# Second-half scores with both heads on 128 partitions, and batch 0's first queries turned on TensorE

## The chip, the cores and the metric

The kernel runs on one core of a Trainium2 chip. The metric is the device time of one execution in microseconds, median of the runs. Of the core's engines TensorE (PE) multiplies matrices into PSUM, VectorE (DVE) and ScalarE (ACT) work on PSUM and SBUF, GpSimd (POOL) on SBUF alone; SyncE (SP) issues most DMAs and all DMA transposes.

## The reference

Attention over 4 batches, 8 heads, 576 positions and 64 columns per head, with a decay from cumulated logarithms of f and a causal mask, then two feed-forward layers over 2304 tokens:

```python
scores = scale * np.matmul(q, k.transpose(0, 1, 3, 2))
cum = np.cumsum(np.log(np.clip(f, 0.0001, 1.0)), axis=-1)
scores = np.where(causal, -1000000000.0, scores + cum[..., :, None] - cum[..., None, :])
attn = np.exp(scores - scores.max(-1, keepdims=True))
x = (attn / (attn.sum(-1, keepdims=True) + 1e-09)) @ v      # heads side by side: 2304 x 512
h = x @ w_in; x = np.maximum(0.01 * h, h) @ w_out           # 512 -> 2048 -> 512
h = x @ w2_in                                               # 512 -> 1024
solu = h * softmax(h)
ln = (solu - mean) / np.sqrt(var + 1e-06) * g_ln
out = ln @ w2_out                                           # 1024 -> 512
```

The weights come in eight bytes per number.

## The kernel before, in words

**Precision.** The feed-forward layers and P·V multiply float16 pairs: each operand is split into a high and a low half, and three products (high·high, high·low, low·high) are summed in PSUM. Scores of a head's first 256 queries ("A" passes, query blocks 0 and 1) are plain float32 matmuls of 66 or 68 rows: 64 of q or k and 2 or 4 of decay. Scores of the other queries ("B" passes: blocks 2 and 3 of 128 queries, and block 4 with the last 64 queries of both heads side by side) use the one-pass type float32r on values split in high and low parts.

**Work of a pair.** A pair is two heads of a batch; there are 16. `prep_full` (L605) loads q and k of an A pass with its decay rows from the DRAM table `dr_d`, in four small DMAs; for batch 0 they are in the tile `qa` from the start. `prep_split` (L621) loads q and k for a B pass with both heads on 128 partitions, and makes for each head two operand tiles `kq`: high parts of one head on one half of the partitions, copies or low parts on the other half, so that one 128-row matmul sums two products, and a 68-row one sums the third and the decay. That takes five copies and subtractions on 64 partitions per head, of 960, 576, 576, 384 and 384 columns. `scores` (L759) multiplies into a `ps_s` bank and takes the row maximum with the mask on VectorE; `softmax` (L717) has ScalarE write exp and its sum, takes the reciprocal, writes float16 halves `hl` of the probabilities, and transposes them by DMA into `pt` (`turn`, L507, on SP). `pv` (L819) multiplies with the float16 halves of V (`split_v`, L692), `evac` (L805) adds the two halves' results into `xr`, and `pair` (L848) splits `xr` into `x`.

**Feed-forward.** Nine blocks of 256 tokens: blocks 0 to 3 are the batches' first 256 positions, 4 to 7 the next 256, 8 the last 64 of all four. A hidden product (`hidden`, L972) needs the block's four pairs in `x`; the output product needs the eight `WO` tiles of its weight group, which share one scale, found by `power` (L667) when all are in. Each weight is loaded into one of three `wst` buffers, joined from its 16-bit parts (L886), bounded and split.

**Order.** All operations go through a planner (`Plan.run`, L187), which lists them with engine, estimated duration, buffers and a due number, and deals them out to the engines in that order when operands and buffers are free; operations with several possible engines get the one that is free first. The program on each engine is the planner's list, and waits are semaphores. `PASSES` gives the due numbers of the A and B passes, `UN` and `ORDER` the order of feed-forward blocks, `LD`, `LDV` and `LDW` how far loads go ahead. There are four `ps_s` banks and one `ps_v` bank.

## Time and profile before

| | us |
|---|---|
| median of 3 runs | 770.1 (768.19 to 773.19) |
| the profiled execution | 769.71 |
| its span, first to last instruction | 767.9 |
| PE busy | 707.0 (92%) |
| DVE, ACT, POOL busy | 529.8, 455.6, 285.0 |

The span is cut into stages below: up to 18 us there are loads and set-up, from 18.0 us scores, from 71.26 us the feed-forward beside attention, from 410 us feed-forward alone.

### The profile page before, as it was taken

How to read it: one execution, taken by the hardware profiler on the slowest of the kernel's cores; microseconds unless marked ns; L12 is line 12 of the kernel's file. 1: busy time of each engine (PE TensorE's matmuls, PEld its weight loads, DVE VectorE, ACT ScalarE, POOL GpSimd, SP SyncE). 2: the span in 40 equal slices, each digit the busy share in tenths (PEclk: the TensorE clock that was granted, in tenths of full speed). 3: DMA queues.
4: the chain of work that ended last, by engine and by line, in shares of the span. 5: the costliest groups of instructions: out<-in, count | busy, mean ns of one | idle time of the engine just before them, and what ended most of it. 6: DMA issues, size and time to landing. Idle time of an engine off the chain costs nothing.

```text
span 767.9 us, 15495 instructions
## 1 busy us (share of the span) xinstructions
PE 707.0 (92%) x5657; PEld 536.9 (70%) x5657; DVE 529.8 (69%) x1343; ACT 455.6 (59%) x1084; POOL 285.0 (37%) x408
## 2 busy tenths in 40 slices
PE   0465889999999999999999999999999999999997
PEld 0244767788888888888889888888875444444443
DVE  6888988776887887677776775212126887778762
ACT  2687999894998779989986576122222332222221
POOL 4546888681766056545551154000002111110110
...
GB/s 239 223 271 207 126 225 210 145 83 139 157 147 144 122 134 130 126 138 131 177 135 115 202 156 29 28 1 15 15 1 83 101 107 109 110 111 82 76 76 82
DMA packets 164139, 94.16 MB, mean 123 GB/s; under 512 B 144368, under 2 KB 144576, under 8 KB 164064
## 3 DMA queue, kind: packets, MB, share of 16 engines
...
q14 instruction: 31, 0.25, 0.1%
...
## 4 chain that ended last, share of the span: by engine, by line
PE 58%; ACT 2%; DMA 2%; DVE 1%; issue 0%; SPq 0%; POOL 0%; ACTq 0%; DVEq 0%
PE ps_f L511 38%; PE ph L511 12%; PE ps_g L511 3%; PE ps_s L511 3%; PE ps_v L511 2%; DMA pt<-hl 1%; ACT ps_s L724 1%; DMA raw<-w2i 1%; ACT hl L465 0%; ACT ps_f L987 0%; ACT xr L808 0%; ACT kq L465 0%; DVE hl L476 0%; ACT ot L1125 0%; ACT junk L662 0%
## 5 line engine op out<-in xcount | busy, mean ns | idle before, releaser
L511 PEld LDWEIGHTS <-wz 128*128 128x128 f16 x2808 | 272.0, 98 | 38.0 <-issue 5.8
L511 PE MATMUL ps_f<-g,wz 128*128 128x256 f16 x780 | 100.8, 273 | 0.0
L476 DVE SCALAR_TENSOR_TENSOR hl<-ps_s,st,hl 128x512 f16<-128x512 f32 (+4 forms) x160 | 82.2, 539 | 22.1 <-ACT hl L465 20.5
L511 PE MATMUL ps_f<-dec,wz 128*128 128x256 f16 x732 | 96.6, 276 | 0.0
L511 PE MATMUL ph<-wy,y 128*128 128x512 f16 x432 | 95.9, 379 | 0.0
L1099 POOL TENSOR_SCALAR s<-s 128x1 f32<-128x1 f32 x18 | 3.4, 190 | 234.5 <-DVE s L1094 215.3
L724 ACT ACTIVATE ps_s<-ps_s,st 128x512 f32<-128x512 f32 (+4 forms) x160 | 78.5, 491 | 19.6 <-DVE st L777 15.6
L480 POOL TENSOR_TENSOR kq<-raw,kq 64x576 fp32r<-64x576 f32 x64 | 77.2, 1209 | 14.0 <-ACT kq L465 8.1
L511 PEld LDWEIGHTS <-tr 128*128 128x128 f16 x432 | 41.9, 98 | 51.4 <-DMA tr<-hl 1.3
L465 ACT ACTIVATE hl<-ps_s,st 128x512 f16<-128x512 f32 (+4 forms) x150 | 73.2, 527 | 7.2 <-DVE st L745 2.6
L511 PEld LDWEIGHTS <-y 128*128 128x128 f16 x432 | 42.1, 98 | 50.3
L511 PE MATMUL ps_v<-pt,VT 128*128 128x128 f16 (+1 forms) x928 | 59.8, 216 | 17.3 <-DMA pt<-hl 8.8
L511 PE MATMUL ps_f<-x,wz 128*128 128x256 f16 x576 | 70.5, 276 | 0.6 <-DVE dec L988 0.6
L511 PEld LDWEIGHTS <-VT 128*128 128x128 f16 x928 | 52.5, 100 | 25.2 <-DMA pt<-hl 10.7
L777 DVE CUSTOM_DVE_ANT_0 ps_s<-ps_s,mask 128x128 f32<-128x128 f32 (+3 forms) x128 | 62.5, 495 | 10.7 <-PE ps_s L511 9.1
L511 PEld LDWEIGHTS <-qa 128*128 128x128 f16 x648 | 62.6, 98 | 8.2 <-issue 0.9
L511 PE MATMUL ps_s<-kq 128*128 128x512 f32 (+5 forms) x256 | 62.1, 369 | 2.7 <-DVE hl L476 2.5
L1082 ACT ACTIVATE raw<-ph,s,ex 128x1024 f32<-128x1024 f32 x18 | 21.6, 1201 | 68.7 <-DVE s L1081 68.0
L988 DVE TENSOR_TENSOR g<-ps_f,g 128x512 f16<-128x512 f32 x37 | 25.5, 689 | 45.4 <-ACT ps_f L987 45.0
L511 PE MATMUL ps_f<-wy,tr 128*128 128x512 f16 x234 | 54.8, 379 | 0.8 <-ACT ot L1125 0.8
L511 PE MATMUL ps_f<-sd,wz 128*128 128x256 f16 x360 | 49.2, 273 | 0.0
L511 PEld LDWEIGHTS ps_s<-kq 128*128 128x128 f32 (+1 forms) x256 | 41.4, 192 | 10.2 <-DVE hl L476 4.6
...
## 6 DMA issues: line engine op xcount, KB each, us to landing
...
VT<-vt SPq DMA_DIRECT2D x16, 320.0 KB
raw<-yp_d SPq DMA_DIRECT2D x18, 256.0 KB
...
out<-ot SPq DMA_DIRECT2D x16, 256.0 KB
raw<-kqa SPq DMA_DIRECT2D x12, 256.0 KB
```

The source lines that it names most:

```text
L465: nc.scalar.activation(o, i, CP, scale=1.0 if scale is None else scale)
L476: nc.vector.scalar_tensor_tensor(o, a, scale, b, op0=ALU.mult, op1=ALU.subtract)
L480: (nc.vector if eng == DVE else nc.gpsimd).tensor_tensor(o, a, b, op=ALU.subtract)
L511: nc.tensor.matmul(o, lhsT=l, rhs=r, start=start, stop=stop)
L724: P.op(ACT, act(W, 1, True) + 93, lambda view=view, j=j, k=k: nc.scalar.activation(view(), view(), AF.Exp, bias=sts.t[:, j:j + 1], scale=- ...
L777: P.op(DVE, dve(W) + 130, lambda i=i, j=j, view=view: nc.vector.tensor_tensor_reduce(view(), view(), mask[:, 512 - 128 * i:640], -0.125, 3 ...
L988: P.op(DVE, dve(512) + 60, lambda: nc.vector.tensor_tensor(g.t[:, 1], ps.t, g.t[:, 0], op=ALU.subtract), eprio, w=[(g, 1)], r=[ps, (g, 0)])
L1082: P.op(ACT, act(1024, 2, True), lambda: nc.scalar.activation(E(), ps.t, AF.Exp, bias=st.t[:, 0:1], scale=ev(SY + blk), accum_out=st.t[:, 1 ...
L1099: nc.gpsimd.tensor_scalar(st.t[:, 5:6], st.t[:, 5:6], 1.0e-6, 1.0, op0=ALU.add, op1=ALU.mult)
```

## The change

- `prep_split` makes one set of three tiles for both heads of a pair, on 128 partitions: high parts, low parts (each in two pieces, 576 and 384 columns), and the decay rows of each head at partitions 0 and 64 of the third tile, whose first 64 rows are zeroed at the start.
- `scores2` replaces `scores` for blocks 2 and 3: for both heads at once, four products (high·high, high·low, low·high, decay) of 64 rows, 4 rows for the decay, alternating between the heads, each head into its own bank. Block 4 takes the same four products on 128 rows.
- `turned` replaces `scores`, `softmax` and `pv` for batch 0's A pass: exp stays in float32 and unnormalised, TensorE multiplies it as stationary operand with a diagonal of the reciprocals, which turns and normalises it, the result is copied to SBUF, and P·V runs in float32 on the unsplit V straight into `x`. `split_v` of batch 0 moves behind its A pass.
- The table `dr_d` is turned by 256 columns, so that an A pass loads its decay rows in one DMA.
- Due numbers, engine choices, block order (`ORDER`, `UN`) and the planner's costs are set anew.

The diff, cut:

```diff
-ORDER = (0, 4, 1, 5, 3, 2, 8, 6, 7)
+ORDER = (0, 1, 4, 5, 3, 2, 6, 8, 7)
 EARLY = 1779.78
 NE = 4
-NQK = 3
+NQK = 2
+KH_ENGS = ("ACT", "DVE", "POOL")
+KL_ENGS = ("DVE", "POOL")
...
-PASSES = (("A", 0, 127.52, 0.5), ("A", 1, 186, 3), ("B", 0, 200, 5), ("A", 2, 222, 8), ("B", 1, 256, 20), ("A", 3, 338, 8), ("B", 2, 373.26, 20), ("B", 3, 454.38, 15.2))
+PASSES = (("A", 0, 127.52, 0.5), ("A", 1, 162.84, 3), ("B", 0, 200, 3.07), ("A", 2, 222, 8), ("B", 1, 234.49, 20), ("A", 3, 338, 8), ("B", 2, 373.26, 20), ("B", 3, 454.38, 15.2))
...
-LD = 11.72
-LDV = 18.49
-LDW = -17.77
+LD = 10.04
+LDV = 8.66
+LDW = -32.78
...
-WSP = (122.0, 192.0)
+WSP = (109.84, 192.0)
...
-UN = ((0, 0), (1, 0), (0, 1), (1, 1))
+UN = ((0, 0), (1, 0), (0, 1), (4, 0), (1, 1), (4, 1))
...
+PTB = (0,)
+DG_ENGS = ("ACT", "DVE", "POOL")
+TE_ENGS = ("ACT", "DVE")
...
+        for k in P.tags["qk"].free:
+            nc.gpsimd.memset(k[2][0:64].bitcast(F32), 0.0)
...
         load((bq, 0), lambda: a(0, 64), lambda: kqa[p].rearrange("(h d) c -> d h c", h=2), 64 * 1024 * 4, prio - LD)
-        for hd in range(2):
-            for c0, k0 in ((0, 0), (256, KB)):
-                load((bq, (hd, c0)), lambda hd=hd, c0=c0: a(64, 68)[:, hd, c0:c0 + 256], lambda hd=hd, k0=k0: dr_d[row(hd, p), :, k0:k0 + 256], 4096, prio - LD,
-                     deps=st["cols"])
-        QK[p] = [[bq]] * 2, lambda hd: a(0, 68)[:, hd], {0: 256, 1: 384}
+        load((bq, 1), lambda: a(64, 68), lambda: dr_d[2 * KD:].rearrange("(h p) t c -> p t h c", h=2)[p - KD, :, :, 0:512], 16384, prio - LD, deps=st["cols"])
+        QK[p] = [[bq]] * 2, lambda hd: a(0, 68)[:, hd], {0: 0, 1: 128}
 
     def prep_split(p, prio):
 
 
-        bufs = []
         N = KB
-        raw = P.buf("raw")
+        raw, bq = P.buf("raw"), P.buf("qk")
         load(raw, lambda: raw.t[:, 0:N], lambda: kq[p, :, 0:N], 128 * N * 4, prio - LD)
         for hd in range(2):
-            bq = P.buf("qk")
-            bufs.append(bq)
-            own, oth = (slice(64 * x, 64 * x + 64) for x in (hd, 1 - hd))
-            T = lambda n, r, c, d, bq=bq: bq.t[n][r, c:d]
-            R = lambda c, d, own=own: raw.t[own, c:d]
-            top = slice(0, 64)
-            copy_f(lambda T=T, own=own: T(0, own, 0, N), lambda R=R: R(0, N), N, prio + PP, w=[(bq, 0)], r=[raw])
-            sub_f(lambda T=T: T(1, top, 0, S), lambda R=R: R(0, S), lambda T=T, own=own: T(0, own, 0, S).bitcast(F32), S, prio + PP,
-                  w=[(bq, "k2")], r=[raw, (bq, 0)])
-            copy_f(lambda T=T, oth=oth: T(0, oth, 0, S), lambda T=T, own=own: T(0, own, 0, S).bitcast(F32), S, prio + PP,
-                   w=[(bq, "k0")], r=[(bq, 0)])
-            copy_f(lambda T=T: T(1, top, S, N), lambda T=T, own=own: T(0, own, S, N).bitcast(F32), N - S, prio + PP,
-                   w=[(bq, "q2")], r=[(bq, 0)])
-            sub_f(lambda T=T, oth=oth: T(0, oth, S, N), lambda R=R: R(S, N), lambda T=T, own=own: T(0, own, S, N).bitcast(F32),
-                  N - S, prio + PP, w=[(bq, "q0")], r=[raw, (bq, 0)])
-            load((bq, "d"), lambda bq=bq: bq.t[1][64:68, 0:N].bitcast(F32), lambda hd=hd: dr_d[row(hd, p), :, 0:N], 16 * N, prio - LD, deps=st["cols"])
-        QK[p] = [[b] for b in bufs], lambda hd: bufs[hd].t, {2: CQ, 3: CQ + 128, 4: CL}
+            load((bq, ("d", hd)), lambda hd=hd: bq.t[2][64 * hd:64 * hd + 4, 0:N].bitcast(F32), lambda hd=hd: dr_d[row(hd, p), :, 256:256 + N],
+                 16 * N, prio - LD, deps=st["cols"])
+        for c, d in ((0, S), (S, N)):
+            copy_f(lambda c=c, d=d: bq.t[0][:, c:d], lambda c=c, d=d: raw.t[:, c:d], d - c, prio + PP, engs=KH_ENGS, w=[(bq, (0, c))], r=[raw])
+            sub_f(lambda c=c, d=d: bq.t[1][:, c:d], lambda c=c, d=d: raw.t[:, c:d], lambda c=c, d=d: bq.t[0][:, c:d].bitcast(F32), d - c, prio + PP,
+                  engs=KL_ENGS, w=[(bq, (1, c))], r=[raw, (bq, (0, c))])
+        QK[p] = [[bq]] * 2, lambda: bq.t, {2: CQ, 3: CQ + 128, 4: CL}
...
-    def split_v(b, prio):
+    def scale_v(b, prio):
         power(EV + 5 * b, KD + 1, [(EX, ("v", KD * b + i)) for i in range(KD)], EB + b, ("b", b), prio)
         inverse(XS + b, ev(EB + b), ("x", b), ("b", b), prio)
+
+    def split_v(b, prio):
...
+    PROD = ((0, 0), (0, 1), (1, 0), (2, 2))
+
+    def qk_both(Q, i, os, k1):
+        _, qk, col = Q
+        t, c0 = qk(), col[i]
+        for n, (x, y) in enumerate(PROD):
+            for hd in range(2):
+                r = slice(64 * hd, 64 * hd + (4 if x == 2 else 64))
+                mm(os[hd], t[x][r, c0:c0 + 128], t[y][r, 0:k1], n == 0, n == 3)
...
+    def scores2(p, i, prio):
+
+        W, pss = 128 * (i + 1), [P.buf("ps_s") for _ in range(2)]
+        P.op(PE, 4 * mmr(W), lambda Q=QK[p]: qk_both(Q, i, [ps.t[:, 0:W] for ps in pss], W), prio, w=pss, r=QK[p][0][0])
+        pts = []
+        for hd, ps in enumerate(pss):
+            sts, view = P.buf("st"), lambda ps=ps: ps.t[:, 0:W]
+            P.op(DVE, dve(W) + 130, lambda sts=sts, view=view: nc.vector.tensor_tensor_reduce(
+                view(), view(), mask[:, 512 - 128 * i:640], -0.125, 3.0e38, ALU.add, ALU.min, sts.t[:, 0:1]), prio + KSTEP * hd, w=[(sts, 0)], rw=[ps])
+            pts.append({i: (softmax([(view, sts, 0, W, [(0, W, 0, W)], ps)], prio + KSTEP * hd), 0)})
+        return pts
...
             def pe(ps=ps, k0=k0, k1=k1, Q=QK[p]):
-                for hd in range(2):
-                    qk_mm(Q, full, 4, ps.t[:, 0:k1 - k0], hd, k0, k1, hd == 0, hd == 1)
+                t, c0 = Q[1](), Q[2][4]
+                for n, (x, y) in enumerate(PROD):
+                    r = slice(0, 68 if x == 2 else 128)
+                    mm(ps.t[:, 0:k1 - k0], t[x][r, c0:c0 + 128], t[y][r, k0:k1], n == 0, n == 3)
 
             n = k1 - k0
-            P.op(PE, 8 * n / 2.4 if full else 4 * mmr(n), pe, prio, w=[ps], r=bq[0] + bq[1], heat=HEAT if full else 1.0)
+            P.op(PE, 4 * mmr(n), pe, prio, w=[ps], r=QK[p][0][0])
...
+    def turned(p, hd, xs, ps_x, prio):
+
+        sts, ps, h = P.buf("st"), P.buf("ps_s"), P.buf("hl")
+        b, kd = divmod(p, KD)
+        vr = RAW[p]
+        f32 = lambda t: (t if len(t.shape) == 2 else t.rearrange("p a n -> p (a n)")).bitcast(F32)
+        at, wide = (0, 128), (128, 256)
+        for i in range(2):
+            P.op(PE, 4 * wide[i] / 2.4, lambda i=i, Q=QK[p]: qk_mm(Q, i, ps.t[:, at[i]:at[i] + wide[i]], hd, 0, wide[i], True, True), prio,
+                 r=QK[p][0][hd], heat=HEAT, w=[(ps, i)])
+        for i in range(2):
+            view = lambda i=i: ps.t[:, at[i]:at[i] + wide[i]]
+            P.op(DVE, dve(wide[i]) + 130, lambda i=i, view=view: nc.vector.tensor_tensor_reduce(
+                view(), view(), mask[:, 512 - 128 * i:640], -0.125, 3.0e38, ALU.add, ALU.min, sts.t[:, i:i + 1]), prio, w=[(sts, i)], rw=[(ps, i)])
+        for i in range(2):
+            P.op(ACT, act(wide[i], 1, True) + 93, lambda i=i: nc.scalar.activation(
+                f32(h.t)[:, at[i]:at[i] + wide[i]], ps.t[:, at[i]:at[i] + wide[i]], AF.Exp, bias=sts.t[:, i:i + 1], scale=-1.0, accum_out=sts.t[:, 3 + i:4 + i]),
+                prio, w=[(sts, 3 + i), (h, i)], r=[(ps, i), (sts, i)])
+
+        def guard():
+            for i in range(2):
+                nc.vector.tensor_scalar(sts.t[:, 6 + i:7 + i], sts.t[:, 3 + i:4 + i], 1.0e-9, None, op0=ALU.add)
+
+        P.op(DVE, 140, guard, prio, w=[(sts, 6)], r=[(sts, 3), (sts, 4)])
+        P.op(DVE, 75, lambda: nc.vector.reciprocal(sts.t[:, 9:11], sts.t[:, 6:8]), prio, w=[(sts, 9)], r=[(sts, 6)])
+        dg, pt, pst = P.buf("pt"), P.buf("pt"), P.buf("ps_f")
+        for i in range(2):
+            copy_f(lambda i=i: f32(dg.t)[:, 128 * i:128 * i + 128], lambda: ident.bitcast(F32), 128, prio, engs=DG_ENGS, scale=lambda i=i: sts.t[:, 9 + i:10 + i],
+                   w=[(dg, i)], r=[(sts, 9)])
+
+        def swap():
+            for i, j, c in ((0, 0, 0), (1, 0, 128), (1, 1, 256)):
+                k = at[i] + 128 * j
+                mm(pst.t[:, c:c + 128], f32(h.t)[:, k:k + 128], f32(dg.t)[:, 128 * i:128 * i + 128], True, True)
+
+        P.op(PE, 3 * 4 * 128 / 2.4, swap, prio + PTP, w=[pst], r=[h, dg], heat=HEAT)
+        copy_f(lambda: f32(pt.t)[:, 0:384], lambda: pst.t[:, 0:384], 384, prio, engs=TE_ENGS, psum=True, w=[pt], r=[pst])
+
+        def pe():
+            for i, j, c in ((0, 0, 0), (1, 0, 128), (1, 1, 256)):
+                mm(ps_x.t[:, 256 * hd + 128 * i:256 * hd + 128 * i + 128], vr.t[:, 128 * j:128 * j + 128], f32(pt.t)[:, c:c + 128], j == 0, j == i)
+
+        P.op(PE, 3 * 4 * 128 / 2.4, pe, prio + AV, w=[(ps_x, hd)], r=[vr, pt], heat=HEAT)
+        x, o, rows = xs[0], xs[1], slice(64 * hd, 64 * hd + 64)
+        src = lambda: ps_x.t[rows, 256 * hd:256 * hd + 256]
+        sc, key = lambda: ev(XS + b)[rows], [(EX, ("x", b))]
+        copy_f(lambda: x.t[rows, 0, o:o + 256], src, 256, prio + AV, engs=TE_ENGS, scale=sc, psum=True, w=[(x, (0, kd, hd))], r=[(ps_x, hd)] + key)
+        sub_f(lambda: x.t[rows, 1, o:o + 256], src, lambda: x.t[rows, 0, o:o + 256], 256, prio + AV, engs=(DVE,), scale=sc, psum=True,
+              w=[(x, (1, kd, hd))], r=[(ps_x, hd), (x, (0, kd, hd))] + key)
...
+        if full and b in PTB:
+            if len(XB.setdefault(b, [])) == kd // 2:
+                XB[b].append(P.buf("x"))
+            ps_x = P.buf("ps_v")
+            for hd in range(2):
+                turned(p, hd, (XB[b][kd // 2], TB * (kd % 2)), ps_x, prio + SM + KSTEP * hd)
+            attn_ops.extend(P.ops[n0:])
+            return
         xr = P.buf("xr")
         k = 0
-        for hd in range(2):
-            pts = {}
-            for unit in UNITS[len(blocks)]:
-                pts.update(scores(p, unit, hd, prio + SM + KSTEP * k, full))
-                k += 1
-            pv(p, hd, pts, xr, prio + AV)
-            if hd == HD4 and 4 in blocks:
-                pv4(p, scores4(p, prio + SM + KSTEP * k, full), xr, prio + AV)
-                k += 1
+        if full:
+            for hd in range(2):
+                pv(p, hd, scores(p, (0, 1), hd, prio + SM + KSTEP * hd), xr, prio + AV)
+        else:
+            both = [{}, {}]
+            for k, i in enumerate(U3):
+                for pts, new in zip(both, scores2(p, i, prio + SM + 2 * KSTEP * k)):
+                    pts.update(new)
+            if not HD4:
+                pv(p, 0, both[0], xr, prio + AV)
+            pt4 = scores4(p, prio + SM + 4 * KSTEP)
+            if HD4:
+                pv(p, 0, both[0], xr, prio + AV)
+            pv(p, 1, both[1], xr, prio + AV)
+            pv4(p, pt4, xr, prio + AV)
...
-                split_v(b, at + PV)
+                scale_v(b, at + PV)
+                if b not in PTB:
+                    split_v(b, at + PV)
             for i in range(KD):
                 pair(KD * b + i, at + step * i, (0, 1) if k == "A" else (2, 3, 4))
+            if k == "A" and b in PTB:
+                split_v(b, at + PV)
```

## Rows read from the trace of the kernel before

**Rows 1.** The page, part 1: busy time, share, instructions.
```profile
PE 707.0 (92%) x5657; PEld 536.9 (70%) x5657; DVE 529.8 (69%) x1343; ACT 455.6 (59%) x1084; POOL 285.0 (37%) x408
```
**Rows 2.** Stages: stretch, length; busy PE, PEld, DVE, ACT, POOL; PEclk, DMA share, GB/s.
```profile
0.00:18.00 18.00, 0.47 (x1) 0.31 (x2) 11.28 (x23) 5.03 (x7) 8.43 (x20) 1.00 0.85 237
18.00:71.26 53.26, 26.98 (x104) 19.15 (x105) 45.02 (x141) 37.75 (x110) 28.79 (x35) 1.00 0.91 251
71.26:110.00 38.74, 33.34 (x280) 27.64 (x279) 34.88 (x100) 36.83 (x90) 32.47 (x33) 1.00 0.56 152
110.00:150.00 40.00, 36.79 (x341) 31.23 (x340) 31.85 (x95) 36.58 (x86) 31.07 (x38) 0.96 0.80 195
...
190.00:410.00 220.00, 216.09 (x2120) 189.26 (x2119) 171.88 (x522) 194.90 (x512) 113.90 (x156) 1.00 0.69 142
```
**Rows 3.** Timeline of PE: start, length, what, count [idle before, releaser].
```profile
18.01 3.33 PE L511 MATMUL ps_s<-qa 66*128 66x128 f32 x10 [0.36 <-DMA qa<-sd]
...
32.38 1.65 PE L511 MATMUL ps_s<-qa 66*128 66x128 f32 x4 [3.23 <-DVE hl L476]
...
66.13 0.80 PE L511 MATMUL ps_v<-pt,VT 128*128 128x128 f16 x6 [0.98 <-DVE xr L811]
...
71.26 4.16 PE L511 MATMUL ps_f<-x,wz 128*128 128x256 f16 x24
...
89.75 5.40 PE L511 MATMUL ps_f<-g,wz 128*128 128x256 f16 x48
```
**Rows 4.** The chain that ended last: start, length, what.
```profile
283.87 2.62 PE ps_f L511 x24
```
**Rows 5.** Timeline of the SP queue: batch 1's decay loads, batch 0's last transposes.
```profile
22.97 6.71 SPq L502 DMA_DIRECT2D raw<-dr_d  x8
...
55.90 2.92 SPq L508 DMA_TRANSPOSE pt<-hl  x2
```
**Rows 6.** Timelines of DVE and ACT between the scores and the first hidden product.
```profile
55.85 0.73 DVE L476 SCALAR_TENSOR_TENSOR hl<-ps_s,st,hl 128x128 f16<-128x128 f32 x2
...
66.93 0.69 DVE L886 SCALAR_TENSOR_TENSOR wz<-wst,wk 128x512 int32<-128x512 int32 x1 [0.45 <-POOL wk L472]
...
70.08 0.15 DVE L654 TENSOR_REDUCE va<-ex 128x1 fp32r<-128x9 f32 x1
...
69.57 0.41 ACT L465 ACTIVATE x<-xr 128x256 f16<-128x256 f32 x1
```
**Rows 7.** Groups of DVE, 0 to 110 us: busy, mean ns, idle before.
```profile
L476 DVE SCALAR_TENSOR_TENSOR hl<-ps_s,st,hl 128x256 f16<-128x256 f32 x16 | 7.6, 475 | 0.2
...
L811 DVE SCALAR_TENSOR_TENSOR xr<-ps_v,xr 64x256 f32<-64x256 f32 x15 | 6.3, 420 | 4.0 <-ACT xr L808 3.8
```
**Rows 8.** Timeline of POOL in the set-up.
```profile
7.07 0.49 POOL L554 TENSOR_SCALAR sd<-sd 8x256 f32<-8x256 f32 x1 [0.71 <-DVE sd L553]
7.61 2.39 POOL L581 MEMSET dec<- 32x576 f32 x4
```
**Rows 9.** The tile kq alone, sum of stages 0 to 410 us, busy by engine.
```profile
sum 410.00, PE 61.54 PEld 41.13 DVE 0.81 ACT 34.35 POOL 113.42; mean PE 10.26 PEld 6.86 DVE 0.14 ACT 5.72 POOL 18.90
```
**Rows 10.** Groups of POOL and ACT that write kq, whole run.
```profile
L480 POOL TENSOR_TENSOR kq<-raw,kq 64x576 fp32r<-64x576 f32 x32 | 45.4, 1420 | 12.8 <-ACT kq L465 8.1 <-POOL st L741 2.6 <-DVE st L745 0.3
L480 POOL TENSOR_TENSOR kq<-raw,kq 64x384 fp32r<-64x384 f32 x32 | 31.9, 998 | 1.1
...
L465 ACT ACTIVATE kq<-kq 64x576 fp32r<-64x576 f32 x22 | 15.0, 682 | 0.7 <-POOL kq L472 0.2
```
**Rows 11.** Waits of PE, whole run, then 0 to 110 us: us, times, longest.
```profile
PE ps_s L511 <- DVE hl L476: 11.0, 9, 3.3
...
PE ps_s L511 <- DVE hl L476: 9.0, 5, 3.3
```
**Rows 12.** Timeline of weight loads (PEld) of a 64-column kq product.
```profile
99.40 0.52 PEld L511 LDWEIGHTS ps_s<-kq 128*128 128x128 f32 x4 [0.21 <-DVE hl L476]
```
**Rows 13.** The page, part 5: weight loads of kq, busy, mean ns.
```profile
L511 PEld LDWEIGHTS ps_s<-kq 128*128 128x128 f32 (+1 forms) x256 | 41.4, 192 | 10.2 <-DVE hl L476 4.6
```

More of the change, by code (lines that the diff above doesn't have):

```diff
@@ L63 @@
 NTR = 3
-YB_ENGS = ("DVE", "ACT")
+PTB = (0,)
+DG_ENGS = ("ACT", "DVE", "POOL")
+TE_ENGS = ("ACT", "DVE")
+PTP = 0.0
+PWL = 500.0
+DMAR = 320.0
+YB_ENGS = ("ACT",)
 VB_ENGS = ("DVE",)
 IB_ENGS = ("DVE",)
-OB_ENGS = ("DVE", "ACT")
-XP = -2.2
-XH_ENGS = ("ACT", "POOL")
+OB_ENGS = ("ACT",)
+XP = -8.31
+XH_ENGS = ("ACT", "DVE", "POOL")
 XL_ENGS = ("DVE", "POOL")
@@ L75 @@
 US0 = 20.0
-HST = 2.5
+HST = 2.59
 TB = 256
@@ L86 @@
 GS = 2.0 ** -24
-YD = 15.51
-OLAG = 33.39
+YD = 17.37
+OLAG = 40.32
 WSC = 256.0
@@ L113 @@
 class Op:
-    __slots__ = ("eng", "dur", "emit", "bufs", "prio", "npred", "succ", "seq", "taken", "dma", "weight", "heat", "lock")
-WEIGHT = {"DVE": 7.07}
-WEIGHT2 = {"DVE": 1.2}
+    __slots__ = ("eng", "dur", "emit", "bufs", "prio", "npred", "succ", "seq", "taken", "dma", "weight", "heat", "lock", "late")
+WEIGHT = {"DVE": 7.06}
+WEIGHT2 = {"DVE": 0.71}
 HEAT = 0.25
-TOPE = 267.42
+TOPE = 268.51
 QUEUES = ("SP",)
-SHARE = 0.54
+SHARE = 0.47
 PORT = 150.0
@@ L126 @@
 HI_ENGS = ("ACT", "DVE")
-UNITS = {2: ((0, 1),), 3: ((3,), (2,))}
+U3 = (3, 2)
 V_ENGS = ("ACT", "POOL")
@@ L194, in run @@
         warm, win, busy = False, 0, 0.0
-        port = 0.0
+        port, ends = 0.0, []
         def push(t, kind, x):
@@ L289, in run @@
                             continue
+                        if o.dma is not None and len(ends) >= 8 and ends[-8] > now:
+                            push(ends[-8], 0, None)
+                            skipped.append(item)
+                            break
                         if locks(o, e) and port > now + PORT:
@@ L333, in run @@
                         end = dma_free + 1000.0
+                        ends.append(end)
                     else:
@@ L338, in run @@
                     push(end, 1, o)
-                    push(end + TOPE, 2, o)
+                    push(end + TOPE + o.late, 2, o)
             if not left:
@@ L441, in body @@
     zrow = zcol.to_broadcast([32, S])
-    P.tag("qk", [tuple(ap.tile([128, KB], F32R, name=f"kq{n}_{j}") for j in range(2)) for n in range(NQK)])
+    P.tag("qk", [tuple(ap.tile([128, KB], F32R, name=f"kq{n}_{j}") for j in range(3)) for n in range(NQK)])
     P.tag("ps_f", tiles(psum, "ps_f", 3, [128, 512], F32))
@@ L501, in move @@
         d = {SP: 475.0, ACT: 490.0, POOL: 1040.0}
-        return flex(engs, [d[e] for e in engs], lambda e: queue[e].dma_start(dst(), src()), prio, dma=nbytes / 360.0, **kw)
+        return flex(engs, [d[e] for e in engs], lambda e: queue[e].dma_start(dst(), src()), prio, dma=nbytes / DMAR, **kw)
     def load(buf, dst, src, nbytes, prio, mode="w", **kw):
@@ L557, in decay @@
         bq = QA[0]
-        for k, r, x, c0 in (("n", 64, n8, 0), ("c", 65, c8, 256)):
+        for k, r, x, c0 in (("n", 64, n8, 256), ("c", 65, c8, 0)):
             move(lambda r=r, c0=c0: qa[r:r + 1, :, :, c0:c0 + 256].rearrange("r h p c -> r (h p) c"), x, 8192, pr,
@@ L579, in decay @@
             T(1, 0, S), c(), -8.0, T32(0, 0, S), op0=ALU.mult, op1=ALU.subtract), [hi])
-        for t, a, b in ((0, CQ, KQ), (1, CQ, KQ), (2, 0, S), (3, 0, S)):
-            step(t, POOL, 500.0, lambda t=t, a=a, b=b: nc.gpsimd.memset(T32(t, a, b), 1.0))
+        for t, a, b in ((0, CQ, KB), (0, KB, KQ), (1, CQ, KB), (1, KB, KQ), (2, 0, S), (3, 0, S)):
+            step(t, POOL, pool1(b - a), lambda t=t, a=a, b=b: nc.gpsimd.memset(T32(t, a, b), 1.0))
         for t in range(2):
@@ L593, in decay @@
                 two(T(t, CL, CQ)), T32(t - 2, 512, S).unsqueeze(1).to_broadcast([32, 2, 64]), -1.0, own(), op0=ALU.mult, op1=ALU.mult), [o])
-        st["cols"] = [move(lambda t=t: dr_d[:, t], lambda t=t: T32(t, 0, KQ), 32 * 4 * KQ, -450, r=[key(t)]) for t in range(4)]
+        st["cols"] = [move(lambda t=t: dr_d[:, t], lambda t=t: tb[t % 2].t[32 * (t // 2):32 * (t // 2) + 32, 0:KQ], 32 * 4 * KQ, -450, r=[key(t)]) for t in range(4)]
     st, QK, VT, QA = {}, {}, {}, {}
@@ L704, in split_v, with qk_mm @@
             VT[p] = v
-    def qk_mm(Q, full, i, o, hd, k0, k1, first, last):
+    def qk_mm(Q, i, o, hd, k0, k1, first, last):
         _, qk, col = Q
-        c0 = col[i]
-        if full:
-            a = qk(hd)
-            mm(o, a[:, c0:c0 + 128], a[:, k0:k1], first, last)
-            return
-        a, b = qk(hd)
-        mm(o, a[:, c0:c0 + 128], a[:, k0:k1], first, False)
-        mm(o, b[0:68, c0:c0 + 128], b[0:68, k0:k1], False, last)
+        a, c0 = qk(hd), col[i]
+        mm(o, a[:, c0:c0 + 128], a[:, 256 + k0:256 + k1], first, last)
+    PROD = ((0, 0), (0, 1), (1, 0), (2, 2))
[6 more added lines that the diff above has]
+                mm(os[hd], t[x][r, c0:c0 + 128], t[y][r, 0:k1], n == 0, n == 3)
     def softmax(parts, prio):
@@ L757, in softmax, with scores @@
         return pt
-    def scores(p, unit, hd, prio, full):
+    def scores(p, unit, hd, prio):
         sts, parts, n, at = P.buf("st"), [], 0, 0
```

31 lines of the change are left out of this document (15 added, 16 removed).

## The prediction

> **What bounds the kernel now.** I read the page first. TensorE is busy 92% of a 767.9 us span and every other engine under 70% [rows 1]; that average hides two kernels. The table of busy time by stage [rows 2] separates them: from 190 to 410 us TensorE is busy 98%, while from 18 to 71.26 us it is busy half the time. Its idle time is 17.5 us up to 18 us, 26.3 us from 18 to 71.26, 5.4 us up to 110, 3.2 us up to 150 and 3.9 us between 190 and 410 us. So the time is TensorE's own work plus what it loses, and nearly all of the loss lies before 110 us. An engine that gets lighter later than that is worth only the few microseconds of stall that it ends.
>
> TensorE's timeline then says what the first 71 us wait for [rows 3]. The scores of batch 0 start at 18.01 us, the last of its eight P·V groups at 66.13 us, and the first matmul of the hidden layer, which needs the whole of batch 0's rows 0 to 255, at 71.26 us. That stretch is at the low clock by the spacing, whatever the granted clock column says: 24 matmuls of 256 columns took 4.16 us there and 2.62 us in steady state [rows 3, 4]. The queue of the transposes shows where the tail comes from [rows 5]: the last split of probabilities in batch 0 ended at 56.6 us (55.85 plus 0.73) [rows 6], the two transposes were issued from 55.90 to 58.82 us, and P·V and the x copy followed at 66.13 and 69.57 us [rows 3, 6]. From the split to the first hidden matmul that is 14.7 us, most of it a transfer amid 251 GB/s of loads [rows 2]. The second gate is the output weights: the last of the first group is joined at 67.6 us, the maximum for their common scale is taken at 70.08, and the first matmul on g starts at 89.75 us [rows 3, 6].
>
> **Batch 0 turned on TensorE.** Per head the change removes one transpose, two splits into float16 halves (0.37 and 0.48 us on VectorE) and the 0.42 us add into xr [rows 6, 7], with the separate x copies. It adds a float32 product with the diagonal, one copy out of PSUM, and P·V in float32. Eight heads times (0.37 + 0.48 + 0.42) is 10 us of VectorE; one 64-row subtraction of 256 columns comes back, priced like the xr add at 0.42, or 3.4 us. In the 53.3 us stretch VectorE is busy 45.0 [rows 2], so this is real room. The splits of batch 0's V also move behind its scores.
>
> TensorE pays. One head's scores are two float32 products, 128 and 256 columns wide, in four instructions: 1.65 us at the low clock [rows 3]. Turning is three products of 128 columns, as many columns, so 1.65 us; so is float32 P·V, in place of 0.80 us. That is 8 x (1.65 + 1.65 - 0.80) = 20 us more in a stretch with 26.3 us free. All of batch 0 is 24 such sets. A set's 1.65 us holds the tail of its last matmul, so 24 back to back are 31 to 40 us. They start 1 us later than now: the two new memsets, 64 x 960, stand on POOL ahead of the negated cumulative sums, which had 0.71 us to spare, and a 32 x 576 or 32 x 512 memset took 0.6 us (four in 2.39) [rows 8], so about 1 us each; that row's DMA is what the first score matmul waited for [rows 3]. The last chain (diagonal, turn, copy, P·V, two x writes) is some 4 us by these rows. So 19 + 31 to 40 + 4 gives 54 to 63; I take 57.5 us, because the sets are issued in a row once transposes no longer separate them. The first hidden matmul moves by -14 us; bounds -8 and -17 (and -20 if the clock rises in that stretch).
>
> Whether the end moves as much depends on the second gate. The first group's 16 weights are joined only at 67.6 us [rows 6], and the change gives their loads a lower place in the queue while batch 1's loads rise. Against that, eight transposes leave the queue and split_wo rises in rank. I keep **-12 us** of the 14; the lower end, where the weights do not move, is a rival below.
>
> **Both heads on 128 partitions.** The copies and splits of second-half q and k cost 34.4 us of ScalarE, 113.4 of POOL and 0.8 of VectorE [rows 9], 148.6 us. Before, each pair has 5,760 columns of them in ten instructions on 64 partitions; now 1,920 in four on 128. By POOL's rows a 576 subtraction is 1.42 us, a 384 one 1.00, and by ScalarE's row a 576 copy is 0.68 [rows 10]; a 384 copy by columns 0.5. So 3.6 us a pair, 58 us in all: 91 us of engine time go. Most of it is POOL's, and most lies after 190 us, under a TensorE that is 98% busy [rows 2]. What it can return there is the stall: TensorE's waits for the split of scores are 11.0 us over the whole run, 9.0 of them before 110 [rows 11]. I take **-2 us** of the 3.9 us after 190, and **-3 us** of the 8.6 us between 71 and 150, where the kq work stands beside the weights' splits.
>
> On TensorE each unit of both heads is eight 64-row matmuls instead of four of 128 and 68 rows. Two prices are not in the trace.
> First, whether two heads' products on different row halves overlap. If they do, eight take the time of four; if not, each pair gains 4 x 512 + 4 x 384 columns, by 2.62 us for 24 x 256 [rows 4] 0.87 + 0.66 = 1.53 us, times 16 pairs **24.5 us**. I take the overlap, since each head's product has its own 64 partitions and its own PSUM buffer, and since in the trace the next float32 weight load already starts beside others (four loads of 0.19 us each in 0.52 us) [rows 12, 13]. The Trainium skill, page "TensorE: Matmul & The Clock Gate", Part 3, says that matmuls in distinct row groups run concurrently; no run here shows it yet.
> Second, the weight loads. Those four loads are thus about 0.11 us apart [rows 12, 13]. Eight take 0.88 us: as long as four slots of 512 columns, 0.22 more than four of 384. That is 16 x 0.22 = **+3.5 us**. The four-row decay product at the end uses another row shape than the 64-row ones. Its cost is bounded by nothing and by one drained matmul, 0.16 us (48 in 5.40 us with the last one's tail, against twice 2.62) [rows 3, 4], at three changes in each of 32 units: 0 to 15 us. I take **+3**, near the lower end, as the 68-row products today follow 128-row ones with no gap. The Trainium skill, page "TensorEngine Tiling (Array Packing)", Key Properties, says that a change of tiling mode drains the engine; by that alone the sum would be up to 12 us higher.
>
> Block 4's eight matmuls per pair stay eight. **Merged loads:** four decay loads per first-half pair become one, 36 issues fewer on SP at 0.84 us (eight in 6.71) [rows 5]. They are issued under feed-forward products or, for batch 1, while batch 0 runs, so I give them nothing; uncovered, batch 1's twelve fewer would be worth 10 us of queue. The reordered blocks and passes change no work.
>
> **Sum.** 769.7 (the profiled execution; the median of the runs is 0.4 above) -12 -2 -3 +3.5 +3 = 759.2; on the median 759.6. I forecast 759.
>
> **Rivals.**
> *Row halves do not overlap* (slower). Place: scores2, from the first second-half pass to 410 us, where TensorE is full [rows 2], so all 24.5 us land on the end; the weight-load term disappears. 759 + 24.5 - 3.5 = 780. It decides as soon as more than half of the products run one after the other: at 14 us it cancels the start's gain. For it: no row shows such a pair; against it: separate partitions and buffers. Chance 0.20.
> *The weights hold the second gate.* g still waits until about 89 us, TensorE idles between the hidden products and the output products, and only 3 us of the start survive, with the stalls of 71 to 150 left. 769.7 - 3 - 2 + 6.5 = 771, no change. For it: loads at 251 GB/s up to 71 us [rows 2] and the lower place of weight loads. Against: the maximum for WO's scale is taken 19.7 us before its first use [rows 3, 6], and that span is vector work, which falls. Chance 0.17.
> *The relief is larger.* Scores, turns and P·V back to back bring the full clock before the hidden layer, its start falls by 20 us, and all stalls up to 150 us go. 769.7 - 20 - 8.6 - 2 + 6.5 = 746. For it: ScalarE and VectorE are busy 95% and 90% from 71 to 110 [rows 2]. Chance 0.18.
>
> **Chances.** The forecast has 0.45, with its own range 750 to 766 from the bounds of the start and of the drains. A change of under 1% (762.4 to 777.8) can't be told from none in this kernel. Faster: three quarters of the forecast's case and the large relief, 0.52. Within 1%: the rest of the forecast's case and most of the weights' case, 0.25. Slower: the serial case and a little of the others, 0.23. The range 745 to 782 reaches from the large relief to the serial case.
>
> **What would show it.** First hidden matmul near 57 us: step one right; near 65 or later, float32 work on a cold TensorE has replaced the transposes. The first matmul on g near 78: second gate moved; near 89, the weights' rival. Eight 64-row matmuls of 512 columns in about 0.9 us: overlap; in 1.8, the serial rival. kq work near 58 us: the vector term. TensorE's idle time after 190 us over 4 us would mean that a new wait, on two score buffers at a time or on one P·V buffer, took the place of the old.

## The result, and the profile after

The changed kernel takes 775.74 us (median of 20 runs, 771.89 to 779.99), the kernel before beside it 770.04 (20 runs, 765.97 to 773.68): a ratio of 1.0068, 95% interval 1.0045 to 1.0091. It is slower by 0.45 to 0.91%. The forecast was 759 and faster, so the sign is wrong; the time lies inside the stated range of 745 to 782. The profiled execution has a span of 773.1 us.

Page, part 1, of the kernel after (it answers to [rows 1]):

```profile
PE 732.3 (95%) x5833; PEld 552.9 (72%) x5833; DVE 514.2 (67%) x1313; ACT 428.3 (55%) x1060; POOL 229.4 (30%) x367
```

VectorE, ScalarE and GpSimd got lighter, and TensorE heavier by 25.3 us. Its idle time is the span less this: 60.9 us before, 40.8 after. The change ended 20.1 us of idle time and paid 25.3 of work for it. The stages of [rows 2] in the kernel after, same columns, show where:

```profile
18.00:71.26 53.26, 41.91 (x184) 35.13 (x183) 42.45 (x158) 46.20 (x136) 41.96 (x47) 0.87 0.84 245
71.26:110.00 38.74, 32.47 (x275) 26.63 (x274) 32.89 (x85) 27.78 (x67) 21.90 (x25) 0.93 0.72 182
110.00:150.00 40.00, 39.24 (x365) 32.45 (x364) 30.90 (x92) 32.52 (x81) 27.12 (x33) 0.94 0.71 148
...
190.00:410.00 220.00, 219.46 (x2152) 185.13 (x2149) 161.67 (x481) 171.12 (x461) 66.08 (x115) 1.00 0.61 130
```

From 18 to 71 us TensorE has 14.9 us more work, VectorE 2.6 less, ScalarE 8.5 more and POOL 13.2 more. From 190 to 410 us the 3.9 idle us are down to 0.5.

TensorE's timeline of the kernel after, with start, length, what, count and [idle before, releaser], answers to [rows 3]:

```profile
16.38 1.62 PE L524 MATMUL ps_s<-qa 66*128 66x128 f32 x4 [16.38 <-DMA qa<-sd]
...
30.11 1.49 PE L524 MATMUL ps_f<-pt,hl 128*128 128x128 f32 x6
...
62.03 1.49 PE L524 MATMUL ps_v<-pt,VT 128*128 128x128 f32 x6
63.88 1.15 PE L524 MATMUL ps_f<-x,wz 128*128 128x256 f16 x9
66.44 0.27 PE L524 MATMUL ps_f<-x,wz 128*128 128x256 f16 x1 [1.41 <-ACT x L478]
66.97 3.14 PE L524 MATMUL ps_f<-x,wz 128*128 128x256 f16 x14 [0.26 <-DVE x L489]
...
71.18 2.79 PE L524 MATMUL ps_f<-x,wz 128*128 128x256 f16 x24
...
77.45 6.96 PE L524 MATMUL ps_f<-x,wz 128*128 128x256 f16 x48
...
86.28 2.13 PE L524 MATMUL ps_f<-g,wz 128*128 128x256 f16 x18
```

The last P·V of batch 0 is at 62.03 us instead of 66.13. But the hidden layer's first set stops after nine matmuls and goes on only at 66.44 us, when the last copy of x has come from ScalarE. The first matmul on g is at 86.28 us instead of 89.75.

That second gate is not the output weights here. The maximum for their scale is taken at 57.02 us instead of 70.08, and GpSimd ends the last of their eight splits at 74.98 us, 11 us before the first matmul on g (in the kernel before 88.27 us, 1.5 us before it):

```profile
73.83 1.15 POOL L493 TENSOR_TENSOR wz<-wz,wz 128x512 f16<-128x512 f32 x1
```

What fills the 22.4 us from the first hidden matmul to the first on g is TensorE's own work: 13.8 us on the four hidden sets (96 matmuls), 4.5 us on scores and P·V put between them, and 4.1 us idle. In the kernel before it is 18.5 us: 11.9, 4.1 and 2.5.

In the chain of waits (start, length, what) the units of both heads are, for 512 and for 384 columns:

```profile
311.49 1.32 PE ps_s L524 x8
...
316.32 1.08 PE ps_s L524 x8
```

and the sum of busy time on the tile kq, up to 420 us (answers to [rows 9]):

```profile
sum 420.00, PE 67.70 PEld 41.83 ACT 6.50 POOL 54.19; mean PE 67.70 PEld 41.83 ACT 6.50 POOL 54.19
```

### The profile page after: what moved, and what is told of

Its sections match the earlier page's. It is cut to its first block, busy times and chain, and to the rows that moved or that the text cites. A ratio compares the mean times of both kernels' runs of the same rounds, so it can differ in the third digit from the quotient of the medians.

```text
span 773.1 us, 15662 instructions
## 1 busy us (share of the span) xinstructions
PE 732.3 (95%) x5833; PEld 552.9 (72%) x5833; DVE 514.2 (67%) x1313; ACT 428.3 (55%) x1060; POOL 229.4 (30%) x367
## 4 chain that ended last, share of the span: by engine, by line
PE 75%; ACT 0%; DVE 0%; issue 0%; ACTq 0%
PE ps_f L524 48%; PE ph L524 12%; PE ps_s L524 7%; PE ps_g L524 4%; PE ps_v L524 4%; DVE VT L489 0%; DVE hl L489 0%; ACT ot L1209 0%; ACT hl L478 0%; ACT wst L478 0%; ACTq L1209 0%; ACTq L478 0%
## 5 line engine op out<-in xcount | busy, mean ns | idle before, releaser
L524 PE MATMUL ps_f<-x,wz 128*128 128x256 f16 x672 | 86.5, 284 | 1.7 <-ACT x L478 1.4
L524 PE MATMUL ps_f<-g,wz 128*128 128x256 f16 x648 | 83.3, 273 | 0.0
L524 PE MATMUL ps_f<-dec,wz 128*128 128x256 f16 x648 | 81.4, 273 | 0.0
L478 ACT ACTIVATE hl<-ps_s,st 128x384 f16<-128x384 f32 (+4 forms) x139 | 69.7, 536 | 14.4 <-DVE st L752 5.1
L524 PE MATMUL ps_v<-pt,VT 128*128 128x128 f16 (+2 forms) x928 | 64.2, 220 | 9.4 <-ACT pt L478 4.0
L524 PE MATMUL ps_f<-sd,wz 128*128 128x256 f16 x420 | 57.3, 273 | 0.0
L524 PE MATMUL ps_f<-wst,wz 128*128 128x256 f16 x420 | 53.9, 273 | 0.0
L524 PE MATMUL ps_s<-kq 64*128 64x512 f32 (+2 forms) x192 | 50.9, 428 | 1.0 <-DVE hl L489 1.0
L798 DVE CUSTOM_DVE_ANT_0 ps_s<-ps_s,mask 128x512 f32<-128x512 f32 (+1 forms) x64 | 39.5, 633 | 13.9 <-PE ps_s L524 13.7
L748 POOL TENSOR_SCALAR st<-st 128x1 f32<-128x1 f32 (+1 forms) x48 | 10.6, 221 | 120.1 <-ACT ps_s L731 119.6
```

What stands on the lines that cost most here:

```text
L478: nc.scalar.activation(o, i, CP, scale=1.0 if scale is None else scale)
L524: nc.tensor.matmul(o, lhsT=l, rhs=r, start=start, stop=stop)
L748: nc.gpsimd.tensor_scalar(scale(), total(), 1.0e-9, PS, op0=ALU.add, op1=ALU.mult)
L798: P.op(DVE, dve(W) + 130, lambda sts=sts, view=view: nc.vector.tensor_tensor_reduce(view(), view(), mask[:, 512 - 128 * i:640], -0.125, 3. ...
```

## The experiments

**Each step alone.** Three kernels take the change apart: without turning, with the older second-half scores, and with neither, which leaves the new due numbers, block order, engine choices and merged loads. A ratio is always to the kernel before run beside it; that one's median lay between 769.92 and 771.64 us, so differences of medians from different experiments are uncertain by 1 to 2 us, and the ratios are the safer comparison.

Without turning:

```diff
-PTB = (0,)
+PTB = ()
```

> The changed kernel with batch 0's first queries done as before (transposes by DMA, float16 P.V); the second-half scores stay new. Theory A (the second-half scores carry the loss, by mode changes on TensorE; turning batch 0 gains): TensorE's lost time before 71 us goes back from 48 to about 59 us, its work falls by 7.5 us, so about 4 us slower than the changed kernel, 779 us (before: 770). Theory B (turning batch 0 carries the loss: float32 work and the low clock until 120 us): 6 us faster than the changed kernel, about 770 us.

Measured: 772.26 us, ratio 1.0011 [0.9989, 1.0033]: faster than the change by 3.5 us, so turning does not gain (theory A had 779).

With the older scores (`prep_split`, block 4, buffers and products as before):

```diff
-NQK = 2
+NQK = 3
...
-    def qk_both(Q, i, os, k1):
+    def qk_two(Q, i, o, hd, k0, k1, first, last):
...
+        mm(o, a[:, c0:c0 + 128], a[:, k0:k1], first, False)
+        mm(o, b[0:68, c0:c0 + 128], b[0:68, k0:k1], False, last)
```

> The changed kernel with the second-half scores and their operands as before (128-row and 68-row products, ten copies a pair); batch 0 stays turned. Theory A: the 32 units lose 0.40 and 0.37 us each of mode changes, 12.3 us of TensorE work, and 3 to 4 us of stalls come back between 190 and 410 us, so about 767 us, below both. Theory B: within 2 us of the changed kernel, about 775 us.

Measured: 767.71 us, ratio 0.9968 [0.9943, 0.9993].

With neither (both diffs):

> Neither of the two steps: the changed kernel's due numbers, block order, engine choices and merged decay loads alone, with old scores everywhere. Theory A: 770 to 772 us, like the kernel before. Theory C (the new due numbers and block order carry the loss): 775 us or more.

Measured: 764.08 us, ratio 0.9911 [0.9879, 0.9942], which neither theory had. So what was costed at nothing gained 6.7 us, turning alone cost 3.6 (767.71 - 764.08), and the new scores alone 8.2 (772.26 - 764.08). The intervals of turning alone and of neither step nearly touch, those of the scores are well apart. The three add up: 764.1 + 3.6 + 8.2 = 775.9, against 775.74. Span, TensorE's busy time (page, part 1) and their difference, for one profiled execution of each:

| kernel | span | busy | idle |
|---|---|---|---|
| before | 767.9 | 707.0 | 60.9 |
| neither step | 763.4 | 708.7 | 54.7 |
| new scores alone | 770.6 | 721.5 | 49.1 |
| turning alone | 767.6 | 718.5 | 49.1 |
| both (the change) | 773.1 | 732.3 | 40.8 |

Each step ends 5.6 us of idle time, and adds 12.8 (scores) or 9.8 us (turning) of TensorE work.

**The merged loads**, in the kernel with neither step, as four DMAs again:

```diff
-        load((bq, 1), ..., dr_d[2 * KD:].rearrange(...)[p - KD, :, :, 0:512], 16384, prio - LD, ...)
+        for hd in range(2):
+            for c0 in (0, 256):
+                load((bq, (hd, c0)), ..., dr_d[row(hd, p), :, c0:c0 + 256], 4096, prio - LD, ...)
```

> Neither of the two steps (as e5), with the decay loads of an A pair in four DMAs again, everything else as in e5. Theory L (the merged loads carry e5's gain of 6.7 us over the kernel before, by 36 issues of 0.84 us on SP): 768 to 770 us. Rival (the new due numbers and block order carry it): 764 to 765 us.

Measured: 766.37 us, ratio 0.9953 [0.9935, 0.9972], beside 0.9911 [0.9879, 0.9942] with one DMA. The intervals overlap, so the 2.3 us for the merging aren't separated from nothing; that due numbers, order and engine choices gain something is, since the interval of 0.9953, without the merging, lies below 1.

**Turns.** The changed kernel with each unit's products issued head by head:

```diff
-        for n, (x, y) in enumerate(PROD):
-            for hd in range(2):
+        for hd in range(2):
+            for n, (x, y) in enumerate(PROD):
```

> The changed kernel with its second-half score products issued head by head (all products of the lower rows, then all of the upper rows) instead of in turns. If the overlap of the two row halves comes from their being issued in turns, it is lost: 384 or 512 columns a second time for two float16 products and the decay product, about 1.5 us in each of the 16 units or 24 us, 800 us. If the halves never ran beside each other (the rival of the prediction, by which pairs only queue), nothing changes: 776 us.

Measured: 810.63 us, ratio 1.0509 [1.0458, 1.0559]. TensorE's timeline, one unit of 512 columns by heads:

```profile
299.96 0.50 PE L524 MATMUL ps_s<-kq 64*128 64x512 f32 x1
300.29 0.62 PE L524 MATMUL ps_s<-kq,kq 64*128 64x512 f32 x2
300.85 0.92 PE L524 MATMUL ps_s<-kq 4*128 4x512 f32 x2
301.61 0.62 PE L524 MATMUL ps_s<-kq,kq 64*128 64x512 f32 x2
302.16 0.50 PE L524 MATMUL ps_s<-kq 4*128 4x512 f32 x1
302.59 0.40 PE L524 MATMUL ps_v<-pt,VT 128*128 128x128 f16 x4
```

and the kernel after, in turns (rows that the view groups overlap each other):

```profile
311.42 0.50 PE L524 MATMUL ps_s<-kq 64*128 64x512 f32 x2
311.75 0.63 PE L524 MATMUL ps_s<-kq,kq 64*128 64x512 f32 x4
312.31 0.50 PE L524 MATMUL ps_s<-kq 4*128 4x512 f32 x2
312.74 0.39 PE L524 MATMUL ps_f<-g,wz 128*128 128x256 f16 x2
```

From the first product to the next other matmul it is 2.63 us by heads and 1.32 in turns. The two row halves do run beside each other, and only when issued in turns: the "serial" rival has its mechanism wrong, and issuing by heads costs 34.9 us. The Trainium skill, page "TensorE: Matmul & The Clock Gate", Part 3, says that matmuls in distinct row groups run concurrently; these rows agree.

**The four-row product.** With the decay product on 64 rows (the third tile zeroed whole), no unit changes its row shape inside; with it second instead of last, each unit changes it once more.

```diff
-                r = slice(64 * hd, 64 * hd + (4 if x == 2 else 64))
+                r = slice(64 * hd, 64 * hd + 64)
```

> The changed kernel with the decay product of scores2 on 64 rows instead of 4 (the third tile is zeroed whole, so the added rows are zero). Theory A with the drain at every change of row shape: one of three changes in each of 32 units goes, about 0.10 to 0.13 us each, so 3 to 4 us faster than the changed kernel, 772 us, and a unit of 512 columns takes about 1.2 us in place of 1.33. Rival: the drain is only between 64-row and 128-row products: no change, 775.7 us, 1.33 us.

```diff
-    PROD = ((0, 0), (0, 1), (1, 0), (2, 2))
+    PROD = ((0, 0), (2, 2), (0, 1), (1, 0))
```

> The changed kernel with the 4-row decay product of scores2 between the 64-row ones instead of last, so one more change of row shape in each of 32 units (four in place of three), with the same products. Theory A (each change costs a drain; taking the 4-row product away saved 0.2 us a unit): 0.1 to 0.2 us more a unit, 3 to 6 us slower than the changed kernel, 779 to 782 us. Rival (the 4-row product costs as such, not by the change of shape): as the changed kernel, 775.7 us.

Measured: 770.69 us (0.9994 [0.9972, 1.0016]) on 64 rows, 782.19 us (1.0166 [1.014, 1.0193]) in the middle. Chain of waits, decay on 64 rows:

```profile
309.58 1.12 PE ps_s L524 x8
...
314.21 0.90 PE ps_s L524 x8
```

and in the middle:

```profile
315.97 1.53 PE ps_s L524 x8
...
321.00 1.29 PE ps_s L524 x8
```

Against 1.32 and 1.08, a unit loses or gains 0.18 to 0.21 us, 32 times: some 6.4 us, and the runs moved by -5.0 and +6.5. One change between 64 and 4 rows costs 0.2 us. The Trainium skill, page "TensorEngine Tiling (Array Packing)", Key Properties, says that a change of tiling mode drains the engine; the rows agree that it costs time.

**The start.** The turning product in float16, in the kernel with turning alone; its low parts are left out. Three instructions of 0.53 us together take the place of the six of 1.49 us above. "One-pass turning" stands for this below.

```diff
-                mm(pst.t[:, c:c + 128], f32(h.t)[:, k:k + 128], f32(dg.t)[:, 128 * i:128 * i + 128], True, True)
+                mm(pst.t[:, c:c + 128], h.t[:, k:k + 128], d16()[:, 128 * i:128 * i + 128], True, True)
```

> Old second-half scores, batch 0 turned (as e3), with the turning product in float16 instead of float32: exp and the diagonal are rounded to float16, the low parts are left out, so the product takes one pass and not four. Theory W (turning costs by its float32 work on TensorE, 7.5 us in all): 3.8 us of that work go, 764 us. Theory G (the first products on g wait for the output weights' scale, and earlier rows of x only lengthen that wait): within 1 us of e3, 767.7 us.

Measured: 761.97 us, ratio 0.99 [0.9876, 0.9925], the lowest median of all, though its interval overlaps that of neither step. The second gate's rival was tried with the output weights loaded earlier, in the kernel with turning alone:

```diff
-LDW = -32.78
+LDW = -17.77
```

> Old second-half scores, batch 0 turned (as e3), with LDW set back from -32.78 to -17.77, so that weight loads keep the place in the queue that they had before. Theory G: the first matmul on g moves from 90.8 us (e3) to 86 or earlier and the kernel gains 3 to 5 us, 763 to 765 us. Theory W: within 1 us of e3, 767.7 us.

Measured: 772.69 us, ratio 1.0037 [1.0017, 1.0058], 5.0 us slower than with the later loads: the first hidden matmul went to 71.44 us and the first on g to 98.18. Earlier weights hurt, against both theories; they are not what was missing.

ScalarE's timeline in the kernel after says why x was late (start, length, what):

```profile
61.04 0.47 ACT L478 ACTIVATE pt<-ps_f 128x384 f32<-128x384 f32 x1
61.50 3.17 ACT L478 ACTIVATE wz<-wz,ex 128x512 f16<-128x512 f32 x5
64.57 1.32 ACT L478 ACTIVATE qa<-wz,ex 128x512 f16<-128x512 f32 x2
65.92 0.47 ACT L478 ACTIVATE x<-ps_v,ex 64x256 f16<-64x256 f32 x1
```

and so in the kernel with turning alone:

```profile
62.97 1.22 ACT L478 ACTIVATE kq<-kq 64x384 fp32r<-64x384 f32 x2
64.22 2.56 ACT L478 ACTIVATE wz<-wz,ex 128x512 f16<-128x512 f32 x4
66.69 1.93 ACT L478 ACTIVATE qa<-wz,ex 128x512 f16<-128x512 f32 x3
68.64 0.47 ACT L478 ACTIVATE x<-ps_v,ex 64x256 f16<-64x256 f32 x1
```

The copy that opens the hidden layer stands behind seven and nine other copies. The P·V that it copies had ended at 63.5 us in both, so it came 2.4 and 5.2 us late. The copies of wz and qa ahead of it in the change are splits of the output weights, whose scale was taken there at 57.02 us and not at 70.08. Three kernels put the copies of x on VectorE: turning alone, the change, and one-pass turning.

```diff
-        copy_f(lambda: x.t[rows, 0, o:o + 256], src, 256, prio + AV, engs=TE_ENGS, ...)
+        copy_f(lambda: x.t[rows, 0, o:o + 256], src, 256, prio + AV, engs=("DVE",), ...)
```

> Turning with the older second-half scores (767.7 us), and the copies that write batch 0's x put on VectorE by hand, where the planner may choose ScalarE otherwise. There the last of them started at 68.64 us, behind copies of kq and of weights that ScalarE had from 62.97 on, and the first hidden products stalled 3.08 us for it. Theory Q, that the place of the x copy in ScalarE's queue kept the start's gain: the hidden products start near 65 us without that stall, and 764 us. Rival, that TensorE's own added work or the weights set the time: the stall goes and comes back behind it, 767 to 768 us.

> The changed kernel (775.7 us) with the copies that write batch 0's x put on VectorE. Its last x copy started at 65.92 us behind seven copies of weights, and the stall was 1.41 us and 0.26. Theory Q: 774 us, and the first hidden products in one piece near 64 us. Rival: 776 us.

> One-pass turning with the older second-half scores (762.0 us; low parts left out of the turning product), and the copies that write batch 0's x put on VectorE. There ScalarE had its last x copy at 61.68 us at once and nothing stalled for it, so theory Q has nothing to take away: 762 us, or 1 to 2 us slower for VectorE's longer queue. Rival, that VectorE is the better place for x whatever the queue: 760 us or less.

Measured: 764.28 us (0.9901 [0.9868, 0.9933]), 773.95 us (1.0028 [1.0006, 1.0049]) and 769.28 us (0.9979 [0.9954, 1.0003]). The second is not separated from the change itself (its interval begins at 1.0045), and the third is above both of its expectations. TensorE's timeline, turning alone with x on VectorE:

```profile
57.70 1.62 PE L524 MATMUL ps_v<-pt,VT 128*128 128x128 f32 x6 [0.24 <-DVE x L489]
...
61.51 5.11 PE L524 MATMUL ps_f<-x,wz 128*128 128x256 f16 x24
...
83.16 3.88 PE L524 MATMUL ps_f<-g,wz 128*128 128x256 f16 x18
```

The hidden layer starts at 61.5 us in one piece, and 3.4 us come off the time (5.2 by the ratios): the place of the x copy in ScalarE's queue was one cause. (The planner deals all later work out anew when an engine is fixed, so this is the queue with what follows from it.) The control went the other way, though its hidden layer started earliest of all:

```profile
58.30 3.07 PE L524 MATMUL ps_f<-x,wz 128*128 128x256 f16 x24
...
100.20 3.30 PE L524 MATMUL ps_f<-g,wz 128*128 128x256 f16 x21
```

and its largest wait of TensorE after the first is (us in total, times, longest):

```profile
PE ps_v L524 <- DVE VT L489: 7.4, 1, 7.4
```

VectorE, with the copies of x on it, brought the split of V late, and TensorE, in order, stood before a P·V with the products on g behind it. With one-pass turning the first hidden matmul moved from 64.16 to 58.30 us and the first on g from 81.35 to 100.20.

**More of it, and both mends.** One-pass turning for batch 1 too (older scores), and the change with the decay on 64 rows and one-pass turning:

```diff
-PTB = (0,)
+PTB = (0, 1)
```

> The older second-half scores with the turning product in float16 (low parts left out of it, as in the run with one-pass turning, 762 us), and the first queries of batch 1 turned on TensorE too. Theory that turning adds TensorE work and pays only while TensorE idles for the transposes: slower than 762, about 766 us. Rival, that the transposing DMAs of batch 1 still hold work back: 760 us or less.

> The changed kernel with both mends: the decay product on 64 rows, and the turning product in float16 (low parts left out of it). If the costs of the two steps add: 775.7 - 5.0 - 5.7 = 765 us. If the two share one cause, so that the second mend finds nothing left, 770 us.

Measured: 768.41 us (0.9969 [0.9941, 0.9996]) and 766.94 us (0.9952 [0.9931, 0.9974]). Turning batch 1 costs 6.4 us on 761.97, and the two mends of the change add up to within 2 us (765 by their sum). The three lowest are not separated from each other: one-pass turning with the older scores, 761.97 us, and, with no part left out, neither step, 764.08, and turning alone with x on VectorE, 764.28. All three beat the kernel before and the change.

## Why the prediction was wrong, by its steps

- **The start, -12: this step failed.** "20 us more in a stretch with 26.3 us free" counted float32 work as covered and let the gates move by 14 and 12 us. TensorE's work came below its price (14.9 us more up to 71 us) and the idle time covered it, but the first hidden matmul came at 63.88 us instead of 57.5 (by -7.4, outside the bounds of -8 and -17), with x whole at about 66.9, and g at 86.28 instead of 78. Alone the step cost 3.6 us. Three things were missing. First, the sum for the first gate held the sets and nothing beside them. From 16.38 to 63.88 us TensorE spent 29.6 us on the 24 sets, less than the 31 to 40 forecast; 6.6 us went to scores of batch 1 that the planner put among them, 2.0 to small products for scales, and 9.4 us it idled, 7.1 of them until ScalarE had written a copy out of PSUM or an exp (us in total, times, longest):

```profile
PE ps_v L524 <- ACT pt L478: 4.0, 2, 3.2
PE ps_s L524 <- ACT hl L840: 2.7, 2, 1.6
```

  ScalarE was not in the sum. These groups are new there between 18 and 71 us (busy, mean ns | idle before), in place of exp and copies that are shorter or fewer:

```profile
L478 ACT ACTIVATE pt<-ident,st 128x128 f32<-128x128 f32 x12 | 4.4, 392 | 0.0
L478 ACT ACTIVATE pt<-ps_f 128x384 f32<-128x384 f32 x8 | 3.8, 481 | 2.2 <-PE ps_f L524 2.1
L478 ACT ACTIVATE x<-ps_v,ex 64x256 f16<-64x256 f32 x8 | 3.7, 460 | 0.1
```

  From 60 to 70 us ScalarE is busy 9.89 of 10 us, before 7.04:

```profile
60.00:70.00 10.00, 8.34 (x42) 6.71 (x42) 7.66 (x22) 9.89 (x28) 9.15 (x11) 0.67 0.77 228
```

  The sets were not issued in a row, as "24 back to back" had it: diagonals, copies out of PSUM and copies of x come between them. The run with x on VectorE gave 3.4 us back. Second, work under idle time is free only where that time would stay idle. With the queue mended, turning alone (764.28) still gains nothing on neither step (764.08), though its first product on g is 4.8 us earlier (87.92 there): in the profiled executions it ends 11.2 us of idle time (43.5 against 54.7) and adds 9.6 us of work (718.3 against 708.7). The float16 product brought 5.7 us (767.71 to 761.97), but in that kernel the hidden layer did not stall for x either, and fixing x on VectorE made it slower. Third, the granted clock, which the prediction let only rise. With neither step and with turning alone it was, from 71.26 to 110 us, 0.96 and 0.86 (the third number from the end):

```profile
71.26:110.00 38.74, 31.87 (x265) 26.54 (x264) 31.96 (x85) 36.47 (x90) 31.16 (x32) 0.96 0.61 164
71.26:110.00 38.74, 34.12 (x275) 28.28 (x274) 33.93 (x94) 32.99 (x77) 26.77 (x29) 0.86 0.63 156
```

  In turning alone the clock fell to the lower level at 68.23 us, inside the stall of 3.08 us for x, and rose at 81.89. From 71.26 us on TensorE worked 11.3 us at the lower level there, 5.7 with neither step (2.3 of them ahead of its first clock record, by the spacing), 10.0 in the change and 7.6 with x on VectorE. A matmul takes twice as long at that level (last section), so half of the first difference, 2.8 us by this estimate from one execution each, could be most of the 3.6. No run holds the clock fixed. So how much of the loss is TensorE's added work, how much the queues and how much the clock is not separated.
- **Stalls, -2 and -3.** TensorE's idle time from 71.26 to 410 us is 12.5 us before, 12.0 with neither step, 6.6 with the new scores alone: the relief of 5 us is there. It came back as work: the step adds 12.8 us of busy time, where the prediction priced 6.5.
- **Row halves overlap.** Right; the rival at 780 for lost overlap was even too cheap (34.9 us, not 21 to 24.5): by heads each unit also changes row shape three times inside and not once, some 13 us at 0.2 us a change, by estimate.
- **Weight loads +3.5 and drains +3: mis-sized.** Together 6.5, and with the stalls of -5 the new scores were to cost 1.5; alone they cost 8.2. All groups of kq products, from the first to the next other matmul, take 53.5 us of work with neither step and 63.0 with the new scores alone, so +9.5 (56.9 and 65.1 with the waits inside). Of the parts, the four-row product, taken at 3 as "near the lower end", is 6.4 by unit and 5.0 by time; the +3.5 of weight loads no run tests by itself. "The 68-row products today follow 128-row ones with no gap" was the wrong row to choose by.
- **Vector work 58 us.** Right: 6.50 + 54.19 up to 420 us, less 1.9 of memsets, is 58.8. As the prediction says of engines off the bound, 90 us less of it bought only stalls.
- **Memsets ahead of the first scores, +1.** Wrong way: the scores start at 16.38 us, not after 18.01.
- **Order and merged loads, 0.** With the engine choices they gained 6.7 us, the only gain in the change. "The reordered blocks and passes change no work" is true and says nothing of time: busy time rose by 1.7 us and idle time fell by 6.2.
- **The rivals.** The measured time lies between the weights' rival (771) and the serial one (780), about as far from each, and neither mechanism is there: the output weights were ready 11 us before the first matmul on g, and the row halves overlap. In the sum, -12 -2 -3 +3.5 +3 = -10.5 should have been +3.6 for turning, +8.2 for the scores with their stalls, and -6.7 for the order: +5.1. The start was off by 15.6 us, the scores by 6.7, and the order, counted at nothing, hid as much again.

That the range held is luck: it reached to 782 for a case that did not occur, and an uncounted gain of 6.7 us kept the time inside. The chance of 0.52 for faster rested on the start.
